# Queries in memory order of 1 KB pieces for batches 0 to 2, scores that read them with a step, and a new order of loads

## The chip, the core and the metric

One NeuronCore of a Trainium2 chip runs the whole program. The metric is the device time of one execution in microseconds (us), as the median of several runs. Engines: TensorE (matrix products, PE in the profile, its weight loads PEld), VectorE (DVE), ScalarE (ACT), GpSimd (POOL), and SP, which here only issues DMA transfers. The profile is one execution; its span is about 2 us below the time measured from outside.

## The reference, cut to what matters

Attention with a position bias over 8 batches of 8 heads, 576 tokens, 64 numbers a head, then layer norm and a two-layer MLP on each token:

```python
scores = scale * np.matmul(q, k.transpose(0, 1, 3, 2))
cum = np.cumsum(np.maximum(s, 0.0), axis=-1)
bias = -(cum[:, :, :, None] - cum[:, :, None, :])
scores = np.where(causal, -1e9, scores + np.minimum(bias, 0.0))
attn = softmax(scores);  x = attn @ v          # heads side by side: (8, 576, 512)
xn = (x - mu) / np.sqrt(var + 1e-06) * g_ln
out = x + np.maximum(xn @ w_ch1, 0.0) @ w_ch2  # 512 -> 2048 -> 512
```

## The kernel before

Heads are counted g = 0 to 63, eight a batch (b = g // 8). For a head, queries and keys are cast to bf16, turned by TensorE through an identity matrix into PSUM (the memory that matmuls write), and copied to `qkT`, with the bias as four extra rows (68 in all). The scores are computed with the keys as the stationary operand (the weight load, PEld in the profile) and the queries as the moving one, whose columns set the spacing of matmuls (in these traces 216 ns for 512 of them, some 30 for 64); ScalarE takes the exponential; TensorE multiplies with the values. The MLP of a finished batch is cut into units that fill TensorE between later heads.

Batches 1 and 2 (`QUADS`) load queries and keys in 1 KB pieces: partition p gets tokens 4p to 4p + 3. After the transposes column t * 128 + p holds token 4p + t, so the copy out of PSUM puts the columns in token order by reading with a step. Batch 0 is loaded in 256-byte pieces and needs no reordering.

```python
QUADS = (1, 2)
...
def t_quads(b, h, engs):                     # batches 1 and 2
    ...
        copy(
            engs[i],                         # queries (i = 0) and keys (i = 1)
            qkT[b][0:DK, i * H + h, 0 : NF * P].rearrange("r (p t) -> r p t", t=NF),
            pts[i][0:DK, 0 : NF * P].rearrange("r (t p) -> r p t", t=NF),
        )
    copy("dve", ..., tails[:, :, 0:TL])      # the last 64 tokens of both
...
def mm(o, kb, lo, hi):                       # scores of key block kb, queries lo to hi
    lhsT = qkT[b][0:DK, H + h, kb * P : (kb + 1) * P]
    ...
        nc.tensor.matmul(o[:, w:], lhsT=lhsT, rhs=qkT[b][0:DK, h, lo + w : hi], start=True, stop=True)

mm(s01[:, 0:512], 0, 0, 512)
mm(s01[:, 512:576], 0, 512, 576)
mm(s01[:, 576:1024], 1, 128, 576)
mm(s23[:, 0:320], 2, 256, 576)
mm(s23[:, 320:512], 3, 384, 576)
mm(pot[:, 448:512], 4, 512, 576)
...
for c, g in enumerate((6, 6, 7, 7)):                    # first weight
    at(g, "a", lambda c=c: load_w1(c))
for h, g in enumerate((0, 0, 1, 1, 7, 7, 8, 8)):        # heads of batch 1
    at(g, "e", lambda h=h: b1_in(h))
for i, g in enumerate((10, 10, 11, 11)):                # second weight
    at(g, "b", lambda i=i: load_w2(i))
```

The softmax here doesn't subtract the row's maximum and nothing guards it: scores larger than these inputs give would overflow.

## Time and profile before

| | before |
|---|---|
| median of 3 runs | 378.04 us (377.99 to 378.38) |
| TensorE busy | 94% of 378.5 us |
| VectorE, ScalarE, GpSimd busy | 53%, 43%, 44% |
| scores of g = 11 / g = 16 / g = 24 exponentiated from | 43.9 / 82.5 / 129.7 us |

TensorE's busy share is nearly all of the span, so what counts is where it is not full.

### The profile page before, as it was taken

What the parts mean: (1) busy time and instruction counts of PE and PEld (TensorE: products, weight loads), DVE (VectorE), ACT (ScalarE), POOL (GpSimd) and SP (SyncE); (2) the same over time, 40 slices, a digit from 0 to 9 for tenths busy, and PEclk for the clock granted to TensorE, in tenths of its full rate; (3) what the DMA queues carried; (4) which work ended last, traced back from release to release, by engine and by line L of the source; (5) the groups of instructions that cost most, each with busy time, mean ns of one, the idle gap of its engine ahead of it and who ended that gap; (6) DMA issues with size and microseconds to landing.
All of it is one profiled execution on the core that took longest, in us unless ns stands there. A gap on an engine that the chain in (4) does not pass through costs nothing.

```text
span 378.5 us, 7931 instructions
## 1 busy us (share of the span) xinstructions
PE 354.7 (94%) x3017; PEld 204.5 (54%) x3017; DVE 201.9 (53%) x466; ACT 163.9 (43%) x295; POOL 167.6 (44%) x328
## 2 busy tenths in 40 slices
PE   6987878888999999999999999999999999899994
PEld 5966645455555455545555755555555555344471
DVE  6788575765454544594447435733555353933131
ACT  3755755154563457335632546444623554031020
POOL 3537964493634545575455544463444111500000
PEclk9998999999999999999999999999999999999998
DMA  9958989997999789999999999599804001420202
GB/s 164 207 150 190 221 143 187 245 248 176 176 227 227 137 198 211 229 198 205 174 210 239 174 246 224 119 195 207 156 29 113 29 2 55 113 55 0 86 28 55
DMA packets 175253, 59.12 MB, mean 156 GB/s; under 512 B 162224, under 2 KB 170416, under 8 KB 175216
## 3 DMA queue, kind: packets, MB, share of 16 engines
q1 hardware_dynamic: 165200, 46.43, 63.5%
q0 software_dynamic: 4224, 4.19, 7.0%
q10 hardware_dynamic: 5792, 8.00, 6.3%
q8 instruction: 23, 0.38, 0.4%
q14 instruction: 14, 0.11, 0.1%
HBM read 37.11 MB, written 9.44 MB: 123 GB/s over the span
## 4 chain that ended last, share of the span: by engine, by line
PE 75%; DMA 11%; DVE 6%; SPq 4%; issue 2%; POOL 1%; ACT 0%; DVEq 0%; POOLq 0%; ACTq 0%
PE ph L373 29%; PE py L384 28%; PE s L217 9%; PE pot L264 6%; DMA ring<-in_q_dram 4%; DMA ring<-in_v_dram 4%; DVE xn L323 2%; SPq L430 2%; DMA ring<-in_k_dram 1%; DVE stats L308 1%; DMA xnT<-xn 1%; SPq L422 1%; SPq L434 1%; DVE x L273 1%; PE pt L186 1%
## 5 line engine op out<-in xcount | busy, mean ns | idle before, releaser
L233 ACT ACTIVATE e<-s 128x1024 bf16<-128x1024 f32 (+1 forms) x128 | 99.0, 808 | 88.0 <-PE s L217 86.2
L384 PE MATMUL py<-w_bf,hT 128*128 128x512 bf16 x576 | 133.4, 379 | 0.0
L373 PE MATMUL ph<-xnT,w_bf 128*128 128x512 bf16 x512 | 120.7, 379 | 1.7 <-DMA xnT<-xn 1.7
L236 POOL TENSOR_SCALAR_AFFINE_SELECT e<-e 128x384 bf16<-128x384 bf16 x104 | 45.7, 464 | 111.2 <-ACT e L233 102.6
L358 DVE TENSOR_SCALAR hT<-ph 128x512 bf16<-128x512 f32 x72 | 49.6, 690 | 77.0 <-PE ph L373 76.4
L373 PEld LDWEIGHTS <-w_bf 128*128 128x128 bf16 x640 | 58.2, 98 | 50.3 <-issue 2.2
L384 PEld LDWEIGHTS <-hT 128*128 128x128 bf16 x576 | 53.1, 98 | 56.1 <-DVE hT L358 0.2
L356 ACT ACTIVATE hT<-ph 128x512 bf16<-128x512 f32 x72 | 43.0, 597 | 79.6 <-PE ph L373 77.3
L217 PE MATMUL s<-qkT 68*128 68x64 bf16 (+5 forms) x320 | 54.5, 287 | 0.0
L127 POOL CAST aug<-ring 128x512 bf16<-128x512 f32 (+2 forms) x85 | 44.4, 547 | 15.0 <-DMA ring<-in_k_dram 7.3
L390 DVE SCALAR_TENSOR_TENSOR yo<-py,rstd,x 128x512 f32<-128x512 f32 x32 | 24.0, 749 | 47.7 <-PE py L384 45.5
L217 PEld LDWEIGHTS <-qkT 68*128 68x128 bf16 x372 | 32.5, 98 | 24.7
L264 PEld LDWEIGHTS <-e 128*128 128x128 bf16 x960 | 37.9, 98 | 13.6 <-POOL e L236 1.1
L264 PE MATMUL pot<-v_bf,e 128*128 128x65 bf16 x960 | 40.1, 194 | 1.4 <-POOL e L236 1.0
L273 DVE TENSOR_TENSOR x<-pot,rinv 128x320 f32<-128x320 f32 x64 | 31.5, 492 | 2.9 <-DMA out_dram<-yo 0.5
L125 DVE COPY qkT<-pt 68x512 bf16<-68x512 bf16 (+2 forms) x49 | 21.9, 468 | 12.5 <-PE pt L166 4.4
L308 DVE BATCH_NORM_STATS2 stats<-x 128x6 f32<-128x256 f32 (+2 forms) x68 | 23.4, 398 | 0.3
L323 DVE SCALAR_TENSOR_TENSOR xn<-x,mv,gln_b 128x512 bf16<-128x512 f32 x32 | 23.2, 766 | 0.0
L127 POOL CAST v_bf<-ring 128x512 bf16<-128x512 f32 (+2 forms) x33 | 19.5, 613 | 2.2 <-DMA ring<-in_v_dram 2.2
L272 DVE RECIPROCAL rinv<-pot 128x5 f32<-128x5 f32 x64 | 12.0, 187 | 15.0 <-PE pot L264 14.9
L329 POOL TENSOR_TENSOR rstd<-rstd,nhalf 128x2 f32<-128x2 f32 x18 | 18.6, 1031 | 1.5
L166 PE MATMUL pt<-ident,aug 128*68 128x128 bf16 x128 | 11.8, 226 | 6.8 <-POOL aug L127 3.1
(78 smaller groups left out, 217.8 us busy)
## 6 DMA issues: line engine op xcount, KB each, us to landing
out_dram<-yo ACTq DMA_DIRECT2D x27, 256.0 KB, 3.3
ring<-in_q_dram SPq DMA_DIRECT2D x20, 256.0 KB, 4.9
ring<-in_k_dram SPq DMA_DIRECT2D x20, 256.0 KB, 4.8
ring<-in_v_dram SPq DMA_DIRECT2D x20, 256.0 KB, 4.3
w_bf<-in_moe_w_ch_dram POOLq DMA_DIRECT2D x8, 512.0 KB, 9.7
ring<-in_k_dram SPq DMA_DIRECT2D x30, 128.0 KB, 4.2
ring<-in_q_dram SPq DMA_DIRECT2D x22, 128.0 KB, 4.7
x<-in_v_dram SPq DMA_DIRECT2D x17, 128.0 KB, 4.0
```

The costliest lines, as they stand in the source:

```text
L127: nc.gpsimd.tensor_copy(out=o, in_=i)
L217: nc.tensor.matmul(o[:, w:], lhsT=lhsT, rhs=qkT[b][0:DK, h, lo + w : hi], start=True, stop=True)
L233: nc.scalar.activation(out=o, in_=i, func=ACT.Exp, scale=scale)
L236: nc.gpsimd.affine_select(out=d, in_=d, compare_op=ALU.is_ge, fill=0.0, base=0, pattern=[[0, d.shape[1]], [1, P]], channel_multiplier=-1,)
L264: nc.tensor.matmul(pot[:, t * D1 : (t + 1) * D1], lhsT=e[:, c : c + P], rhs=v_bfs[b % 2][:, kb, h, :], start=(kb == 0), stop=(kb == t),)
L273: nc.vector.tensor_tensor(out=xs[b][:, :, h * D : (h + 1) * D], in0=pv[:, :, 0:D], in1=rv.to_broadcast([P, NT, D]), op=ALU.mult,)
L308: nc.vector.bn_stats(out=sts[c, a][:, part, :], in_=x_of(c, a)[:, lo:hi])
L323: eng.scalar_tensor_tensor(out=xn[:, j, :], in0=x_of(c, a), scalar=mv[:, j, 0:1], in1=gln_b, op0=ALU.subtract, op1=ALU.mult,)
L356: nc.scalar.activation(out=o, in_=i, func=ACT.Relu)
L358: nc.vector.tensor_scalar_max(out=o, in0=i, scalar1=0.0)
L373: nc.tensor.matmul(ph[:, j * tok : (j + 1) * tok], lhsT=w1_bf[:, kd, fb * P : (fb + 1) * P], rhs=xnT[c][:, :, kd, :], start=(kd == 0), sto ...
L384: nc.tensor.matmul(st["py"], lhsT=st["h"][:, fb, a * P : (a + 1) * P], rhs=w2_bf[:, fb, :], start=(fb == 0), stop=(fb == FB - 1),)
```

## The change

Its intent: batch 0 too in 1 KB pieces, which the DMA moves faster; spare VectorE the strided copy of the queries by letting TensorE read them in token order straight from the unordered columns; load batch 1 whole before the weights take the DMA; spread g over the partitions by a matmul rather than a broadcast load; issue the fifth score block after the next head's transposes. As the last 64 tokens stay in order, the score matmuls are also cut at token 512. The warm-up spin (matmuls on the identity matrix at the start that only keep TensorE busy) becomes fewer and wider matmuls, 11 of 512 columns for 44 of 128.

```diff
-    QUADS = (1, 2)
+    QUADS = (0, 1, 2)
...
+            if i == 0:
+                copy(engs[0], o[:, 0:S], pt[0:DK, 0:S])
+            else:
+                copy(engs[1], o[:, 0 : NF * P].rearrange("r (p t) -> r p t", t=NF), ...)
+                copy(engs[2], o[:, NF * P : S], pt[0:DK, NF * P : S])
...
+        def queries(lo, hi):
+            qT = qkT[b][0:DK, h, :]
+            if b in QUADS and hi <= NF * P:
+                qT = qT[:, 0 : NF * P].rearrange("r (t p) -> r p t", t=NF)
+                return qT[:, lo // NF : hi // NF]
+            return qT[:, lo:hi]
...
-        mm(pot[:, 448:512], 4, 512, 576)
+        return lambda: mm(pot[:, 448:512], 4, 512, 576)
...
-    spin(44)      # warm-up matmuls of 128 columns
+    spin(11)      # of 512 columns
...
+    def spread_g():
+        pg = ps_m.tile([P, 512], F32, name="pg", tag="pm")
+        nc.tensor.matmul(pg, lhsT=ones_r, rhs=gln_r, start=True, stop=True)
+        nc.vector.tensor_copy(out=gln_b, in_=pg)
...
-    for c, g in enumerate((6, 6, 7, 7)):
+    for c, g in enumerate((7, 7, 8, 8)):
         at(g, "a", lambda c=c: load_w1(c))
-    for h, g in enumerate((0, 0, 1, 1, 7, 7, 8, 8)):
+    for h, g in enumerate((1, 1, 1, 1, 3, 3, 3, 3)):
         at(g, "e", lambda h=h: b1_in(h))
-    for i, g in enumerate((10, 10, 11, 11)):
+    for i, g in enumerate((9, 9, 10, 10)):
         at(g, "b", lambda i=i: load_w2(i))
```

In `queries`, neighbours in the order of reading lie 128 elements, 256 bytes, apart.

More of the change, by code (lines that the diff above doesn't have):

```diff
@@ L97 @@
     xnT_tail = const.tile([P, 2, KD, P], BF16, name="xnT_tail")
+    gln_r, ones_r = xts[0][0:1, :], xts[2][0:1, Dm - P : Dm]
     scr = xbufs[0]
@@ L106 @@
     nc.sync.dma_start(out=s_sb, in_=s.rearrange("b h s -> (b h) s"))
+    nc.gpsimd.dma_start(out=gln_r, in_=moe_g_ln.rearrange("(o f) -> o f", o=1))
+    nc.gpsimd.memset(ones_r, 1.0)
     staged = {}
@@ L161, in t_quads @@
     def t_quads(b, h, engs):
-        pts = [ps_m.tile([P, 2 * 512], BF16, name="pt", tag="pm") for _ in range(2)]
-        tails = pts[1][0:DK, NF * P : NF * P + 2 * P].rearrange("r (j n) -> r j n", j=2)
         for i in range(2):
-            for p in range(NF):
+            pt = ps_m.tile([P, 2 * 512], BF16, name="pt", tag="pm")
+            o = qkT[b][0:DK, i * H + h, :]
+            for p in range(NT):
                 nc.tensor.transpose(
-                    pts[i][0:DK, p * P : (p + 1) * P], aug[:, p, i * H + h, 0:DK], ident
+                    pt[0:DK, p * P : (p + 1) * P], aug[:, p, i * H + h, 0:DK], ident
                 )
-            nc.tensor.transpose(tails[:, i, :], aug[:, NF, i * H + h, 0:DK], ident)
-            copy(
-                engs[i],
-                qkT[b][0:DK, i * H + h, 0 : NF * P].rearrange("r (p t) -> r p t", t=NF),
-                pts[i][0:DK, 0 : NF * P].rearrange("r (t p) -> r p t", t=NF),
-            )
-        copy(
-            "dve", qkT[b][0:DK, :, NF * P : S].rearrange("r (j h) n -> r j h n", j=2)[:, :, h, :],
-            tails[:, :, 0:TL],
-        )
-    def t_pe(b, h, engs=("dve", "dve")):
-        if b in QUADS:
-            return t_quads(b, h, engs)
-        for j, eng in ((h, engs[0]), (H + h, engs[1])):
-            pt = ps_m.tile([P, 2 * 512], BF16, name="pt", tag="pm")
-            for p in range(NT):
-                nc.tensor.transpose(pt[0:DK, p * P : (p + 1) * P], aug[:, p, j, 0:DK], ident)
-            copy(eng, qkT[b][0:DK, j, :], pt[0:DK, 0:SP_])
+            if i == 0:
+                copy(engs[0], o[:, 0:S], pt[0:DK, 0:S])
+            else:
+                copy(
+                    engs[1], o[:, 0 : NF * P].rearrange("r (p t) -> r p t", t=NF),
+                    pt[0:DK, 0 : NF * P].rearrange("r (t p) -> r p t", t=NF),
+                )
+                copy(engs[2], o[:, NF * P : S], pt[0:DK, NF * P : S])
     def t_dma(b, p):
@@ L203, in score_mms @@
         pots[g] = (pot, s01, s23)
+        def queries(lo, hi):
[4 more added lines that the diff above has]
+            return qT[:, lo:hi]
         def mm(o, kb, lo, hi):
             lhsT = qkT[b][0:DK, H + h, kb * P : (kb + 1) * P]
-            w = 0
+            cuts = {lo, hi}
+            if b in QUADS and lo < NF * P:
+                cuts.add(min(hi, NF * P))
             if g < NPM and lo == kb * P:
-                w = min(P, hi - lo)
-                nc.tensor.matmul(
-                    o[:, 0:w], lhsT=lhsT, rhs=qkT[b][0:DK, h, lo : lo + w], start=True, stop=False
-                )
-                nc.tensor.matmul(
-                    o[:, 0:w], lhsT=ident, rhs=negm[:, 0:w], start=False, stop=True
-                )
-            if lo + w < hi:
-                nc.tensor.matmul(
-                    o[:, w:], lhsT=lhsT, rhs=qkT[b][0:DK, h, lo + w : hi], start=True, stop=True
-                )
+                cuts.add(min(hi, lo + P))
+            cuts = sorted(cuts)
+            for c0, c1 in zip(cuts[:-1], cuts[1:]):
+                d = o[:, c0 - lo : c1 - lo]
+                m = g < NPM and c0 == kb * P
+                nc.tensor.matmul(d, lhsT=lhsT, rhs=queries(c0, c1), start=True, stop=not m)
+                if m:
+                    nc.tensor.matmul(
+                        d, lhsT=ident,
+                        rhs=negm[:, 0 : c1 - c0],
+                        start=False, stop=True,
+                    )
         mm(s01[:, 0:512], 0, 0, 512)
@@ L491, in spin @@
         for _ in range(n):
-            nc.tensor.matmul(idle[:, 0:P], lhsT=ident, rhs=ident, start=True, stop=True)
-    spin(44)
+            nc.tensor.matmul(
+                idle, lhsT=ident,
+                rhs=ident.rearrange("p (o n) -> p o n", o=1).to_broadcast([P, 4, P]),
+                start=True, stop=True,
+            )
+    spin(11)
     nc.vector.tensor_scalar(
@@ L501 @@
     )
-    pc = ps_m.tile([P, 512], F32, name="pc", tag="pm")
+    NQ = len(QUADS) * H
+    pq = ps_m.tile([P, 512], F32, name="pq", tag="pm")[:, 0 : NT * NQ]
+    pq = pq.rearrange("p (t c) -> p t c", t=NT)
+    cum_q = cum[0:NQ, 0 : NF * P].rearrange("c (p t) -> c t p", t=NF)
     for p in range(NT):
-        nc.tensor.transpose(pc[:, p * BH : (p + 1) * BH], cum[:, p * P : (p + 1) * P], ident_f)
+        nc.tensor.transpose(
+            pq[:, p, :], cum_q[:, p, :] if p < NF else cum[0:NQ, NF * P : SP_],
+            ident_f[0:NQ, 0:NQ],
+        )
     c8, r8 = (
@@ L507 @@
     )
-    pc_v = pc[:, 0 : NT * BH].rearrange("p (t c) -> p t c", c=BH)
     def split(lo, hi, eng, a=None, o=None):
@@ L521 @@
     cast_head("k", 0, 0, "pool")
-    split(0, H, nc.vector, pc_v[:, :, 0:H], aug[:, :, H:HD, D1:DK])
+    split(0, H, nc.vector, pq[:, :, 0:H], aug[:, :, H:HD, D1:DK])
     nc.scalar.activation(
@@ L527, with cum_all @@
     cast_head("k", 0, 1, "pool")
-    spin(8)
-    t_pe(0, 0, ("act", "dve"))
-    nc.scalar.copy(out=c8, in_=pc_v)
-    def cum_quads():
-        pq = ps_m.tile([P, 512], F32, name="pq", tag="pm")[:, 0 : NF * 3 * H]
-        pq = pq.rearrange("p (t c) -> p t c", t=NF)
-        cum_q = cum[0 : 3 * H, 0 : NF * P].rearrange("c (p t) -> c t p", t=NF)
-        for p in range(NF):
-            nc.tensor.transpose(pq[:, p, :], cum_q[:, p, :], ident_f[0 : 3 * H, 0 : 3 * H])
-        qs = slice(QUADS[0] * H, (QUADS[-1] + 1) * H)
-        nc.vector.tensor_copy(out=c8[:, 0:NF, qs], in_=pq[:, :, qs])
+    spin(2)
+    t_quads(0, 0, ("act", "dve", "act"))
+    nc.scalar.copy(out=c8[:, :, 0:NQ], in_=pq)
+    def cum_all():
+        pc = ps_m.tile([P, 512], F32, name="pc", tag="pm")
+        pc_v = pc[:, 0 : NT * BH].rearrange("p (t c) -> p t c", c=BH)
+        for p in range(NT):
+            nc.tensor.transpose(pc_v[:, p, :], cum[:, p * P : (p + 1) * P], ident_f)
+        nc.vector.tensor_copy(out=c8[:, :, NQ:BH], in_=pc_v[:, :, NQ:BH])
+    def spread_g():
+        pg = ps_m.tile([P, 512], F32, name="pg", tag="pm")
+        nc.tensor.matmul(pg, lhsT=ones_r, rhs=gln_r, start=True, stop=True)
+        nc.vector.tensor_copy(out=gln_b, in_=pg)
     cast_head("q", 0, 2, "dve")
@@ L567, in t_next @@
     def t_next(g):
-        t_pe((g + 2) // H, (g + 2) % H, ("dve", "act" if g >= H else "dve"))
-    at(0, "a2", lambda: t_pe(0, 1))
-    at(0, "a2", cum_quads)
+        t_quads((g + 2) // H, (g + 2) % H, ("dve", "act" if g >= H else "dve", "dve"))
+    at(0, "a2", lambda: t_quads(0, 1, ("dve", "dve", "dve")))
+    at(1, "c", cum_all)
+    at(3, "c", spread_g)
     at(2, "c", lambda: split(H, 2 * H, nc.vector))
@@ L589, in b1_in @@
     def b1_in(h):
-        if h == 2:
-            nc.sync.dma_start(out=gln_b, in_=moe_g_ln.partition_broadcast(P))
         heads_in(1, (h,))
@@ L605, in t_act @@
     def t_act(b, h):
-        t_pe(b, h, ("dve", "act"))
+        t_quads(b, h, ("dve", "act", "dve"))
     def c_head(b, h):
@@ L630 @@
         at(6 + p, "e", lambda p=p: nc.gpsimd.memset(aug[:, p, :, DK:P], 0.0))
+    B2 = 12
     def b2_in(g):
-        if g == 12:
+        if g == B2:
             for what in "qkv":
                 tails_in(what, 2, nc.sync)
-        heads_in(2, range(3 * (g - 12), min(H, 3 * (g - 12) + 3)))
-    for g in (12, 13, 14):
+        heads_in(2, range(3 * (g - B2), min(H, 3 * (g - B2) + 3)))
+    for g in (B2, B2 + 1, B2 + 2):
         at(g, "a", lambda g=g: b2_in(g))
@@ L711 @@
         if g < NG:
-            score_mms(g)
+            score_tail = score_mms(g)
             run(g, "a2")
+            score_tail()
             score_exp(g, 0)
```

## The prediction

> **What bounds the kernel now.** I read the page's slices first, then the matmuls in order of time, then the groups with shapes kept apart, then the DMA packets stretch by stretch.
>
> The slices (40 of 9.46 us each; a digit is the busy share in tenths):
> ```profile
> PE   6987878888999999999999999999999999899994
> DMA  9958989997999789999999999599804001420202
> ```
> From slice 11 (95 us) to slice 34 TensorE is full, and so is nearly all of the rest. Only the first ten slices have holes, and there DMA is full too, except in slices 3, 5 and 10. All the change's parts lie in batches 0 to 2 (heads g = 0 to 23), so the time can only be won or lost before some 95 us, and, where TensorE itself gets more work, up to g = 23.
>
> The holes, from the matmuls in order of time (start us, length us, then idle before and who ended it):
> ```profile
> 9.36 0.22 PE L210 MATMUL s<-qkT 68*128 68x128 bf16 x1 [1.13 <-ACT qkT L123]
> ...
> 32.69 0.41 PE L166 MATMUL pt<-ident,aug 128*68 128x128 bf16 x4 [1.30 <-POOL aug L127]
> ...
> 39.77 0.41 PE L166 MATMUL pt<-ident,aug 128*68 128x128 bf16 x4 [0.68 <-POOL aug L127]
> ...
> 44.09 1.89 PE L373 MATMUL ph<-xnT,w_bf 128*128 128x512 bf16 x8
> ...
> 56.50 0.38 PE L166 MATMUL pt<-ident,aug 128*68 128x128 bf16 x4 [1.95 <-DVE hT L358]
> ...
> 58.17 0.71 PE L264 MATMUL pot<-v_bf,e 128*128 128x65 bf16 x15 [0.96 <-POOL e L236]
> ...
> 73.83 0.40 PE L340 MATMUL ptx<-ident,xn 128*128 128x128 bf16 x4 [0.99 <-DVE xn L323]
> ...
> 91.92 0.38 PE L166 MATMUL pt<-ident,aug 128*68 128x128 bf16 x4 [1.34 <-DVE qkT L125]
> ```
> Scores of g = 0 start at 9.36, of g = 5 at 21.12, of g = 6 at 23.25: 2.13 to 2.3 us a head. Then g = 7 at 27.05, 8 at 29.29, 9 at 33.56, 10 at 37.37, 11 at 42.99. The extra 8 us there are waits for GpSimd's casts, which wait for batch 1's data. The MLP starts at 44.09. g = 16 starts at 80.43.
>
> A head of batch 0 costs TensorE 0.97 us of scores (9.36 to 10.33), 0.56 us of ten transposes and 0.46 us of values: 1.99 of its 2.13 us. So batch 0 already runs at TensorE's pace; DMA (24 loads of 128 KB, done by 20 us) is just behind.
>
> **What the skill says.** "DMA: Bandwidth & Descriptors", section "Why small descriptors are slow (HBM only)", gives a 256-byte descriptor 11 bus cycles for 8 of data, 27% overhead. The trace agrees in direction and shows more: in 10 to 20 us a 256-byte packet takes 20.8 ns (7777 packets) and a 1024-byte one 49.8 to 55 ns, so 1 KB costs 83 ns in small packets and some 52 in one.
> "TensorE: Matmul & The Clock Gate", section "Back-to-back issue gap", has N/2.4 + 2.5 ns warm. The trace agrees: eight 512-column matmuls take 1.73 us to the next one's start, 216 ns each.
> "SBUF — State Buffer", section "Specifications (TRN2)", says of the 16-byte lines "need ≥2 hits per line for full bandwidth; each cross to a new line pays a penalty". The new scores read one query, step 256 bytes, read the next: one hit per line. The kernel before has no strided moving operand, but it has a strided stationary one:
> ```profile
> 5.73 0.49 PE L504 MATMUL pc<-x 64*128 64x64 f32 x5 [0.18 <-DVE x L498]
> ...
> 10.98 0.65 PE L538 MATMUL pq<-x 24*128 24x24 f32 x4
> ```
> Taking off the last one's own length (223 and 272 ns), the contiguous loads follow each other every 0.066 us, and those with a step of 16 bytes every 0.12 us, though they have fewer rows and fewer columns to stream. That is twice as long and fits 128 reads at half of 2.4 GHz. No run yet shows it for a moving operand.
>
> **The change, part by part.**
>
> *Batch 0 in 1 KB pieces.* Its 16 q and k loads of 128 KB go from 512 packets x 20.8 ns / 16 = 0.67 us to 128 x 52 / 16 = 0.42 us: 4 us of DMA. Batch 0 is held by TensorE and the queue's issue (some 0.55 us a load), so its own pace gains nothing; batch 1 can start some 2 to 3 us sooner. The first scores wait on ScalarE's cast of head 1 and copy of head 0; the load lands some 0.6 us sooner, but the key's chain (a strided VectorE copy, then a tail copy) is 0.2 to 0.4 us longer. I take 9.3 us for the start, no gain.
>
> *The copies out of PSUM.* The groups (count | busy us, mean ns):
> ```profile
> L125 DVE COPY qkT<-pt 68x512 bf16<-68x512 bf16 x18 | 12.2, 681 | 4.6 <-PE pt L166 4.4
> L125 DVE COPY qkT<-pt 68x640 bf16<-68x640 bf16 x15 | 6.7, 481 | 3.8 <-PE pt L186 3.7
> L125 DVE COPY qkT<-pt 68x128 bf16<-68x128 bf16 x16 | 3.5, 217 | 4.1 <-ACT qkT L123 4.1
> ```
> A strided copy takes 681 ns, a plain one of 640 takes 481. Batch 0's heads go from two plain copies (0.96 us) to a plain one of 576 (0.44), a strided one and a tail (0.2): 1.32 us. With reciprocal and multiply (0.68) VectorE has 2.0 us a head by summed means, some 1.8 when the overlap of neighbours is taken off. It comes close to being the bound in g = 0 to 10 but does not pass 2.5 us. From g = 8 on a head saves VectorE 0.24 us.
>
> *Scores by strides.* Of a head's 1600 columns 1280 lie below token 512 (512 + 384 + 256 + 128) and are read with the step. At full speed they are 1280 / 2.4 = 0.53 us; at half speed 1.07. So +0.53 us a head if the rule seen on the stationary side holds here, 12.8 us of TensorE for 24 heads, and nothing if it doesn't. The cuts at token 512 add two 64-column matmuls a head in batch 0 (three from g = 12), some 5 ns each, as a 65-column one takes 0.46 / 15 = 31 ns against 27 of columns: 0.3 us in all.
>
> *Batch 1 ahead of the weights.* Before, heads 4 to 7 are issued from 32.05 to 43 us, beside the first weight (issued at 33.0), and the last value tile is waited for until 51.6. After, 30 loads at 0.53 us follow batch 0's directly: issued some 16 to 33 us, head 0 landed near 21, head 4 near 31, head 7 near 36. TensorE wants head 0 at g = 6 (23 to 26 us) and head 4 at g = 10 (36). So these waits go. The first weight is then issued at about 28, the second at about 36; 13.4 us of DMA each (2048 packets x 105 ns / 16), done near 44 and 58. Batch 2, whose tails wait for the last cast of batch 1 (at 55.46 before), starts near 42 and has all landed by about 71 instead of 80.
>
> *The fifth score block after the transposes*, and g by a matmul: the first takes away waits of 0.1 to 0.4 us on VectorE's multiply; the second costs one fp32 matmul (0.9 us estimated as four passes of 512 columns) and one 0.69 us PSUM copy, and removes a 256 KB load.
>
> **The sum.** With the penalty, TensorE's work for g = 0 to 10: 2.6 + 2.8 (the 40-column cumulative sums) + 2.5 + 3.35 (g) + 5 x 2.5 + 2.5 + 3.4 (x transposes) = 29.7 us, so g = 11 at 39.0, and 40.5 with VectorE's stalls: 2.5 us gained. From g = 11 to 18 the waits of 0.96 (GpSimd behind a late value tile), 0.99 (VectorE behind a late query of batch 2) and part of 1.34 and 0.67 go: 3.5 gained. The 1.95 stays: it is VectorE's split of batches 2 to 7. Lost: 5 x 0.53 = 2.65 in g = 11 to 15, and 3.5 to 4.2 in g = 16 to 23, where TensorE is the bound. Total about 0: 378 us.
> Without the penalty, g = 11 comes at about 38 (VectorE and TensorE nearly equal), 5 us gained, plus the same 3.5: 369.5 us.
>
> **The rivals.** (1) *The step is free for moving operands.* For it: separate read paths for moving and stationary data, and nothing in the trace of a strided moving read. Against: the doubled stationary loads, and the skill's line on cache lines. It gives 367 to 372. (2) *The step costs double and TensorE's gain is eaten*: 375 to 381, the likelier one, about 0.7. (3) *VectorE becomes the bound of batch 0* through the three copies: g = 5 at 23 or later and 2 to 3 us of the gain lost even without a penalty, 371 to 374. Against it: 0.6 us of VectorE idle per head before. (4) *The transfers are late anyway*: the early second weight shares DMA with batch 2, so q and k of batch 2 are not sooner than TensorE gets there; then the 3.5 us shrink to 1 to 2. For it: DMA is at 9 in most of slices 4 to 12.
>
> **Range and chances.** Weighing 378 at 0.7 and 369.5 to 372 at 0.3 gives 376. The range 369.5 to 380.5 spans both cases with 2.5 us outside either middle where I think it likely. 2% is 7.6 us, that is below 370.5: only rival 1 in its better half, with nothing lost to VectorE: 0.24. Slower by over 2% needs a step worse than double: 0.04.
>
> **What would show it.** Right: the 68x384 and 68x512 score matmuls last 0.16 to 0.21 us longer, and a head's scores 1.47 us instead of 0.97 (g below 12), 1.22 instead of 0.68 (from 12); no waits over 0.3 us on GpSimd's casts between g = 6 and 11; g = 11 between 38 and 41; the last batch 1 value cast by 40, not 52; strided PSUM copies of queries gone. Wrong: if score matmuls keep their lengths, the result is below 372; if g = 5 starts after 24 with TensorE idle behind VectorE, rival 3; if GpSimd or VectorE still wait for batch 2's loads at g = 15, rival 4.

## The result, and the profile after

The changed kernel takes 412.56 us (median of 4 runs, 411.94 to 413.48) against 378.21 us beside it: the ratio is 1.0907, with a 95% interval of 1.0878 to 1.0935. It is slower by 9%. Here and below a ratio is the mean time of one kernel's runs over that of the other's from the same rounds, so it is not quite the ratio of the medians. Executions over 1.5% slower than the fastest of the same kernel are left out of the means.

The slices of the changed kernel's page (40 of 10.28 us; PEclk is the clock granted to TensorE, in tenths of full speed):

```profile
PE   7999999998999999999999999999999999989995
PEclk9557999999999999999999999999999999999998
```

The holes in TensorE's first ten slices are nearly gone, as intended, and yet all is later. TensorE is not waiting: it is busy for 397 us instead of 355. The second row shows a thing that I had not foreseen: the clock is at half from slice 2 to some way into slice 4 (9.2 to 36.5 us), while TensorE is full.

The groups of score matmuls with their shapes kept apart, before and after (count | busy us, mean ns | idle before):

```profile
L217 PE MATMUL s<-qkT 68*128 68x512 bf16 x52 | 19.8, 381 | 0.0
L217 PE MATMUL s<-qkT 68*128 68x384 bf16 x12 | 4.1, 343 | 0.0
```

```profile
L216 PE MATMUL s<-qkT 68*128 68x512 bf16 x52 | 27.6, 531 | 0.0
L216 PE MATMUL s<-qkT 68*128 68x384 bf16 x24 | 19.6, 816 | 0.0
L216 PE MATMUL s<-qkT 68*128 68x256 bf16 x24 | 14.4, 599 | 0.0
L216 PE MATMUL s<-qkT 68*128 68x448 bf16 x40 | 14.1, 351 | 0.0
```

The 384-column matmuls went from 343 to 816 ns. The 512-column group mixes 12 stepped ones with the 40 of batches 3 to 7: if those 40 stayed at 381, the 12 took (52 x 531 - 40 x 381) / 12 = 1031 ns. The 448-column ones, now only of batches 3 to 7 and without a step, kept their 351.

One head of batch 1 in TensorE's order of time, after and before (start us, length us):

```profile
71.26 2.45 PE L216 MATMUL s<-qkT 68*128 68x512 bf16 x8
73.55 0.19 PE L216 MATMUL pot<-qkT 68*128 68x64 bf16 x1
73.58 1.89 PE L376 MATMUL ph<-xnT,w_bf 128*128 128x512 bf16 x8
```

```profile
47.69 0.82 PE L217 MATMUL s<-qkT 68*128 68x512 bf16 x5
48.34 0.19 PE L217 MATMUL pot<-qkT 68*128 68x64 bf16 x1
```

From the first score matmul to the fifth block the head takes 2.29 us, and took 0.65: 1.64 us more, at full clock, beside the same MLP units (eight of 512 columns in 1.73 us to the next start, as before). 24 heads make 39 us of added TensorE work (an estimate from this head; heads below g = 12 are cut differently, and one at full clock, g = 7, takes 2.5 us from its first score matmul to the transposes, where such a head of e2 below takes 0.9).

The progress of four kernels, as the start of ScalarE's first exponential of a head in their profiles (us). The last two columns are of experiments told below:

| head | before | after | same reads without the step (e2) | queries by copies (e8) |
|---|---|---|---|---|
| g = 0 | 10.1 | 11.5 | 10.7 | 10.2 |
| g = 8 | 30.1 | 49.0 | 31.0 | 30.7 |
| g = 11 | 43.9 | 61.1 | 41.2 | 41.7 |
| g = 16 | 82.5 | 103.4 | 75.5 | 75.5 |
| g = 24 | 129.7 | 162.2 | 121.8 | 122.1 |
| span | 378.5 | 411.3 | 371.2 | 373.2 |

The loss of 32.5 us is complete at g = 24, and from there to the end the kernel before and the changed one both need 249 us.

### The profile page after: what moved, and what is told of

It reads as the page before. It is cut to its first block, busy times and chain, and to the rows that moved or that the text cites. A ratio compares the mean times of both kernels' runs of the same rounds, so it can differ in the third digit from the quotient of the medians.

```text
span 411.3 us, 7966 instructions
## 1 busy us (share of the span) xinstructions
PE 397.2 (97%) x3014; PEld 214.4 (52%) x3041; DVE 199.2 (48%) x474; ACT 164.9 (40%) x296; POOL 168.4 (41%) x331
## 4 chain that ended last, share of the span: by engine, by line
PE 89%; DVE 5%; POOL 1%; issue 1%; DMA 1%; ACT 1%; ACTq 0%; DVEq 0%; POOLq 0%
PE ph L376 30%; PE py L387 25%; PE s L216 20%; PE pot L267 7%; PE pt L170 4%; DVE xn L326 1%; PE idle L495 1%; DVE stats L311 1%; DMA xnT<-xn 1%; PE s L218 1%; DVE yo L393 1%; POOL aug L131 1%; ACT e L236 1%; DVE x L276 1%; PE pg L554 0%
## 5 line engine op out<-in xcount | busy, mean ns | idle before, releaser
L387 PE MATMUL py<-w_bf,hT 128*128 128x512 bf16 x549 | 130.8, 381 | 1.4
L216 PE MATMUL s<-qkT 68*128 68x64 bf16 (+7 forms) x428 | 95.4, 358 | 0.8 <-DVE qkT L129 0.8
L216 PEld LDWEIGHTS <-qkT 68*128 68x128 bf16 x492 | 45.1, 105 | 59.9 <-issue 30.7
L267 PE MATMUL pot<-v_bf,e 128*128 128x65 bf16 x960 | 41.2, 197 | 0.0
L129 DVE COPY qkT<-pt 68x576 bf16<-68x576 bf16 (+2 forms) x56 | 20.2, 383 | 31.2 <-PE pt L170 25.2
L170 PE MATMUL pt<-ident,aug 128*68 128x128 bf16 x240 | 21.2, 246 | 1.7 <-DVE qkT L129 1.0
L170 PEld LDWEIGHTS <-aug 128*68 128x68 bf16 x240 | 18.3, 132 | 4.2 <-issue 1.8
L275 DVE RECIPROCAL rinv<-pot 128x5 f32<-128x5 f32 x64 | 12.0, 187 | 14.5 <-PE pot L267 14.4
```

What stands on the lines that cost most here:

```text
L170: nc.tensor.transpose(pt[0:DK, p * P : (p + 1) * P], aug[:, p, i * H + h, 0:DK], ident)
L216: nc.tensor.matmul(d, lhsT=lhsT, rhs=queries(c0, c1), start=True, stop=not m)
L267: nc.tensor.matmul(pot[:, t * D1 : (t + 1) * D1], lhsT=e[:, c : c + P], rhs=v_bfs[b % 2][:, kb, h, :], start=(kb == 0), stop=(kb == t),)
L387: nc.tensor.matmul(st["py"], lhsT=st["h"][:, fb, a * P : (a + 1) * P], rhs=w2_bf[:, fb, :], start=(fb == 0), stop=(fb == FB - 1),)
```

## The experiments

Theory A: the step in the moving operand costs TensorE about four times the time per column, and the half clock is a consequence. Theory B: the new warm-up spin leaves the clock at half, and the step carries only part of the loss. (That spin has as many columns, and its first part runs for 4.6 us where the old one ran for 4.0.) A third possibility was that VectorE's three copies a head hold up batch 0; the changed kernel's own list of waits speaks against it, with 1.8 us of TensorE's waits for these copies up to g = 24.

**The same matmuls without the step (e2).** Instruction for instruction the changed kernel; only the addresses of the moving reads differ. Its results are wrong; the bias is set to zero so that the exponentials stay finite.

```diff
-                return qT[:, lo // NF : hi // NF]
+                return qkT[b][0:DK, h, lo:hi]
```

> The changed kernel, instruction for instruction, but the scores read the same number of queries without the step (and the bias terms are set to 0 so that nothing overflows): wrong on purpose. Theory A (the step costs about four times the time per column, and TensorE's half clock from 9 to 36 us is only its consequence): 366 to 374 us, score matmuls of 512 columns back to 381 ns from 531, the clock full from some 6 us on. Theory B (the new, shorter warm-up spin leaves the clock at half, and the step itself costs only part of the loss): the clock still at half from 9 to about 36 us and 376 to 390 us.

Measured: 374.51 us (372.94 to 375.92; ratio to before 0.9906, interval 0.9868 to 0.9944). The step is worth the whole loss: the medians differ by 38.1 us and the profiles' spans by 411.3 - 371.2 = 40.1 (e2's profile is of its fastest run), against 39 us from 24 heads at 1.64. The lengths are back:

```profile
L216 PE MATMUL s<-qkT 68*128 68x512 bf16 x52 | 19.8, 381 | 0.0
L216 PE MATMUL s<-qkT 68*128 68x384 bf16 x24 | 7.9, 329 | 0.0
```

The time is just above the range that theory A gave; for the step the mechanism was A's. Of the clock A had said "full from some 6 us on"; it was at half for 3.4 us (10.3 to 13.8), not 27. The table also shows how the lost time adds up. At g = 8 the changed kernel is 18.0 us behind this one: 8 heads x 1.64 = 13 us, and 5 us more, while its clock is at half. At g = 24 it is 40.4 us behind, 39 of which are the step. So the half clock cost some 5 us in batch 0 by this estimate. That so little of it shows at g = 24 fits with TensorE's waits: from 9 us to g = 24 they sum to 7.6 us in e2 and to 3.8 in the changed kernel.

**The old spin in the changed kernel (e3).**

```diff
-    spin(11)     # and spin(2), of 512 columns
+    spin(44)     # and spin(8), of 128 columns
```

> The changed kernel with the warm-up spin of before (44 and 8 matmuls of 128 columns). Theory A: the clock is still at half from about 9 to 36 us, 409 to 413 us. Theory B: the clock stays full and the time falls by 6 us or more, to 400 to 406 us.

Measured: 412.25 us (two runs), no change. Windows of 10 us of the changed kernel, then of this one (busy us of each engine, then the granted clock, the DMA share and GB/s):

```profile
10.00:20.00 10.00, 10.00 (x84) 7.55 (x82) 4.10 (x11) 3.48 (x6) 6.17 (x15) 0.50 0.86 216
20.00:30.00 10.00, 10.00 (x86) 7.47 (x86) 5.64 (x16) 3.47 (x6) 5.62 (x14) 0.50 0.69 179
```

```profile
10.00:20.00 10.00, 10.00 (x89) 6.61 (x88) 4.32 (x12) 3.42 (x6) 6.54 (x16) 0.83 0.85 216
20.00:30.00 10.00, 10.00 (x83) 6.37 (x82) 5.47 (x15) 3.42 (x6) 6.08 (x14) 0.58 0.75 193
```

The old spin moves the half-clock stretches about (this profile has another from 59.2 to 62.6) but doesn't end them; TensorE counts as busy for the full 10 us in all four. With e2, which has the new spin and only 3.4 us of half clock, theory B falls. This profile also prices the half clock: 10.2 us less of it before g = 8 puts that head 2.2 us ahead of the changed kernel, and g = 24 still 2.1.

What lets the clock fall is not shown, and so A's second half is not shown either. The longest stretches at half lie in stepped matmuls of batch 0 (27 us in the changed kernel, 17 here and in e7 below). But the changed kernel is back at full clock from 36.5 us, while its stepped matmuls go on to g = 23, with only 3.4 us more at half; and shorter stretches come without any step, such as 6.8 us in e10 and 10.2 us in e4's copy of the kernel before, ahead of its probes.

**The price of a step by itself (e4).** The kernel before, with matmuls of 512 columns behind its end that read the first weight in several ways.

```diff
+    quad = flat[:, 0:512].rearrange("p (t n) -> p n t", t=4)
+    pair = flat[:, 0:512].rearrange("p (t n j) -> p n t j", t=4, j=2)
+    # 12 x flat[:, 0:512]; then 6 each of steps 2, 4, 8, 16, of quad, of pair, and step 1 again:
+    nc.tensor.matmul(probe, lhsT=ident, rhs=..., start=True, stop=True)
```

> The kernel before with matmuls of 512 columns put behind its end, which read a bf16 operand with a step of 1, 2, 4, 8, 16 elements, in fours 256 bytes apart as the changed scores do, and in pairs of neighbours 256 bytes apart. Only the spacing of these matmuls counts, not the time of the kernel. If what counts is one hit per 16-byte line: 216 ns for steps 1, 2 and 4, some 850 ns (four times) for 8, 16 and the fours, about half of that for the pairs. If any step costs: 850 ns for step 2 and 4 too. If the cost comes from hopping among four places: the fours alone are slow.

The order of time, one line for each kind (start us, length us; L735 is step 1, L737 step 2, L739 step 4, L741 step 8, L743 step 16, L745 the fours of the change, L747 pairs, L749 step 1 again):

```profile
371.82 2.75 PE L735 MATMUL probe<-w_bf,ident 128*128 128x512 bf16 x12
374.41 1.52 PE L737 MATMUL probe<-w_bf,ident 128*128 128x512 bf16 x6
375.77 2.87 PE L739 MATMUL probe<-w_bf,ident 128*128 128x512 bf16 x6
378.46 5.58 PE L741 MATMUL probe<-w_bf,ident 128*128 128x512 bf16 x6
383.86 5.69 PE L743 MATMUL probe<-w_bf,ident 128*128 128x512 bf16 x6
389.36 5.36 PE L745 MATMUL probe<-w_bf,ident 128*128 128x512 bf16 x6
394.55 2.80 PE L747 MATMUL probe<-w_bf,ident 128*128 128x512 bf16 x6
397.17 2.67 PE L749 MATMUL probe<-w_bf,ident 128*128 128x512 bf16 x6
```

From the start of one matmul to the next, in the middle of each group (single records of the trace, which the lines merge): 216 ns for step 1, 227 for step 2, 452 for step 4, 900 for step 8, 918 for step 16, 864 for the fours, 437 for the pairs. So neither "any step costs" (step 2 is nearly free) nor "one hit per line" (step 4 has two elements in 16 bytes and costs double) as I had written it. What fits is a price for each 16-byte line that the read turns to: step 8 turns to 512 lines in 900 ns, 1.76 ns a line; step 4 to 256, which gives 450; step 2 to 128, 225; step 1 to 64, 113, which hides behind the 216 that 512 columns take anyway. The clock was at half from 382.6 us on, and step 8 took 900 ns on either side of that; the fours took 864 here, at half, and 864 again in the next experiment at full clock: the price does not depend on TensorE's clock. It also explains the changed kernel: (2.29 - 4 x 0.03 for the unstepped blocks in that time) / 1280 columns = 1.70 ns a column, close to the fours' 864 / 512 = 1.69.

**The rule put to the test (e9).** Another set behind the same kernel: pairs, runs of four neighbours, a step of 3; then stationary operands, contiguous and with a step of 8.

```diff
+    runs4 = flat[:, 0:512].rearrange("p (t n j) -> p n t j", t=4, j=4)
+    # ... 6 x pairs, runs4, flat[:, 0:1536:3]; then, with 64 moving columns:
+    nc.tensor.matmul(probe[:, 0:64], lhsT=flat[:, 0:128], rhs=ident[:, 0:64], start=True, stop=True)
+    nc.tensor.matmul(probe[:, 0:64], lhsT=flat[:, 0:1024:8], rhs=ident[:, 0:64], start=True, stop=True)
```

> The kernel before with another set of matmuls behind its end: 512 columns read in pairs of neighbours 256 bytes apart, in runs of four neighbours 256 bytes apart, with a step of 3 elements; then 64-column matmuls whose stationary operand of 128 bf16 columns is contiguous, and with a step of 8 elements; then plain ones and the fours again. If a moving read costs some 1.75 ns for each 16-byte line it turns to (900 ns / 512): pairs 448 ns at full clock, runs of four 224 or the plain 216, step 3 (192 lines) some 336. If any break in the run costs, runs of four are well above 216. The stationary operand: 31 ns contiguous; 120 ns with the step if it goes at the rate of the fp32 loads of the kernel before (128 reads), 224 if at the moving operand's.

In order of time (L736 pairs, L738 runs of four, L740 step 3, L742 and L744 the stationary operands, L746 step 1, of which the trace lacks the first record, L748 the fours):

```profile
371.57 2.78 PE L736 MATMUL probe<-w_bf,ident 128*128 128x512 bf16 x6
374.18 1.51 PE L738 MATMUL probe<-w_bf,ident 128*128 128x512 bf16 x6
375.53 2.20 PE L740 MATMUL probe<-w_bf,ident 128*128 128x512 bf16 x6
377.56 0.52 PE L742 MATMUL probe<-ident,w_bf 128*128 128x64 bf16 x12
377.91 0.91 PE L744 MATMUL probe<-ident,w_bf 128*128 128x64 bf16 x12
378.88 1.24 PE L746 MATMUL probe<-w_bf,ident 128*128 128x512 bf16 x5
379.96 3.61 PE L748 MATMUL probe<-w_bf,ident 128*128 128x512 bf16 x4
```

Start to start, at full clock: pairs 437 ns (448 expected), runs of four 222 (224), step 3 340 (336). The rule holds in all three. With the stationary operand the matmuls follow each other after 29 ns, and after 62 with a step of 8: twice as long, and only 0.5 ns for each of the 128 columns loaded. (The 64 moving columns alone take 27 ns at 216 for 512, so the 29 may be theirs and not the load's.) Neither of the two values that I had expected came, but it shows why my prediction could not carry the price over: the same step that makes this spacing 2.1 times as long makes that of a moving read 4.2 times as long.

**The change without the step: queries by strided copies (e1, e8).** All of the change stays except that VectorE orders the queries again, as it did in batches 1 and 2.

```diff
-                copy(engs[0], o[:, 0:S], pt[0:DK, 0:S])
+            copy(engs[i], qkT[b][0:DK, i * H + h, 0 : NF * P].rearrange("r (p t) -> r p t", t=NF), ...)
+        copy(engs[2], ..., tails[:, :, 0:TL])
...
-            if b in QUADS and hi <= NF * P:
+            if False:
```

> The changed kernel, but the queries are put in order by the strided copy out of PSUM, as batches 1 and 2 had it before, and the scores read them without a step; all else of the change stays (right results). Theory A: the loss goes and the rest of the change shows its worth: 368 to 376 us, the clock full from 6 us. Rival (VectorE becomes the bound of batch 0 with two strided copies a head): 376 to 382 us, with TensorE waiting on VectorE's copies in g = 1 to 6. Theory B: half clock until some 36 us and 380 to 390 us.

Measured: correct, median of the five fast runs 375.68 us (375.71 with the slow one), ratio of the fast runs 0.9906 (0.9874 to 0.9937). The profiled run took 952 us: in it a head with four MLP units took 12.5 us instead of 4.6, with TensorE busy throughout and no clock change on record. It was run again:

> The kernel of e1_query_copies once more, because its profile fell in a run of 952 us. Expected: 373 to 376 us as its five other runs, TensorE's work for a head of batch 1 or 2 as in the kernel before (0.68 us of scores), and VectorE nearly full in g = 0 to 10 if it is what now bounds that stretch. If the 952 us come again, they belong to the kernel and not to the chip's state.

Measured: 374.27 us (373.68 to 376.68), ratio 0.9894 (0.9863 to 0.9925), and no run like the odd one in six. So this version beats both kernels, the kernel before by 1% (clear of noise, but under the 2% that counts as faster here). What may keep it from gaining more is in the windows (columns as above, VectorE the third):

```profile
20.00:30.00 10.00, 8.68 (x162) 7.59 (x160) 9.84 (x28) 6.73 (x12) 7.65 (x16) 1.00 0.81 189
30.00:40.00 10.00, 6.86 (x128) 6.00 (x126) 9.77 (x31) 7.08 (x13) 9.10 (x16) 1.00 1.18 205
```

VectorE is busy for 9.8 of 10 us from 20 to 40 us. TensorE's waits between 9 and 122 us are now mostly for VectorE (the longest in total of this kernel, then of the kernel before to 130 us; us, times, longest):

```profile
PE pot L218 <- DVE x L278: 3.4, 5, 1.5
PE pt L170 <- DVE qkT L129: 1.4, 2, 1.0
```

```profile
PE pt L166 <- POOL aug L127: 3.1, 5, 1.3
PE pt L166 <- DVE hT L358: 1.9, 1, 1.9
```

GpSimd's casts, which waited for data, are gone from TensorE's list. VectorE took their place. The waits of the two full lists together fall from 14.4 to 8.9 us, 5.5 less, and the spans differ by 5.3.

**The order of loads alone (e5)**, in the kernel before:

```diff
-    for c, g in enumerate((6, 6, 7, 7)):
+    for c, g in enumerate((7, 7, 8, 8)):
-    for h, g in enumerate((0, 0, 1, 1, 7, 7, 8, 8)):
+    for h, g in enumerate((1, 1, 1, 1, 3, 3, 3, 3)):
-    for i, g in enumerate((10, 10, 11, 11)):
+    for i, g in enumerate((9, 9, 10, 10)):
```

> The kernel before with nothing but the new order of loads (batch 1 whole from g = 1 and 3, the weights at g = 7 and 8, and 9 and 10). If the order is what the change gains: 374 to 376 us, with the waits on GpSimd's casts in g = 7 to 11 mostly gone. If the gain needs batch 0's 1 KB pieces first (batch 1 cannot start sooner than 18 us): 376.5 to 378.5 us, the waits at g = 6 and 7 still there.

Measured: 376.21 us, ratio 0.9939 (0.9912 to 0.9967). In its profile g = 11 comes at 41.3 and g = 16 at 77.3, against 41.7 and 75.5 with all the rest. More than half of the gain seems to be the order; the rest of the change together (1 KB pieces of batch 0, fifth block, spin, g) adds what remains, by times whose intervals overlap.

**g by a DMA again (e6)**, in the version with copies (the load of the kernel before is put back, the matmul and its copy taken out):

```diff
-    at(3, "c", spread_g)
+        if h == 2:
+            nc.sync.dma_start(out=gln_b, in_=moe_g_ln.partition_broadcast(P))
```

> The kernel of e1_query_copies, but g is spread by a DMA again as before. If spreading g by TensorE costs its two fp32 matmuls (some 1 us at full clock) and its 0.68 us copy on the path of batch 0: 0.8 to 1.5 us faster than e8, 372.5 to 375 us. If those lie beside waits, or the 256 KB load delays batch 1 by as much: within 0.4 us of e8.

Measured: 375.58 us, ratio 0.9918 (0.9895 to 0.9940), against 0.9894 for e8. The expected gain of a microsecond did not come. The two intervals overlap, so I can only say that spreading g by TensorE costs nothing that shows.

**The step in batch 0 alone (e7)**, batches 1 and 2 by copies:

```diff
+    STEP = (0,)
-            if b in QUADS and hi <= NF * P:
+            if b in STEP and hi <= NF * P:
```

> The step only in the scores of batch 0, batches 1 and 2 by strided copies as in e1. If every head pays the same 1.6 us: 8 x 1.6 = 13 us over e8, 387 to 390 us. If batch 0 has slack for it (VectorE's copies, waits for data): 380 to 385 us. The clock at half for much of 10 to 35 us if the stepped matmuls cause it.

Measured: three runs of 388.07, 391.51 and 393.89 us (a fourth, of 394.04, slow), ratio 1.0333 (1.0277 to 1.0389). The profiled run is the fastest, with a span of 386.3 us, 13.1 over e8's 373.2. That this is just 8 heads x 1.64 is partly luck: at g = 24 it is 15.1 us behind e8, with 17 us of half clock where e8 had none, and the rest of e8's profile has 3.4 us of half clock that this one has not. The other runs lie above the 390 that I had allowed. They have no profile, but their granted clock falls as the time grows: 0.974 in the profiled run, 0.959 at 391.51, 0.956 at 393.89. So batch 0 did not hide the step, as my second guess had it: TensorE's listed waits up to g = 24 only fall from 8.9 us in e8 to 7.5.

**Taking load off VectorE (e10, e11, e12).** In the version with copies, the key copy goes to ScalarE from g = 4, or from g = 1, instead of g = 8:

```diff
-        t_quads((g + 2) // H, (g + 2) % H, ("dve", "act" if g >= H else "dve", "dve"))
+        t_quads((g + 2) // H, (g + 2) % H, ("dve", "act" if g >= 4 else "dve", "dve"))
```

> The kernel of e1/e8 with the strided key copy on ScalarE from g = 4 instead of g = 8. In e8 VectorE is busy for 9.8 of 10 us from 20 to 40 us and TensorE waits on its multiply. If VectorE bounds that stretch: four copies of 0.6 us less, g = 11 some 2 us sooner, 372 to 373.5 us against e8's 374.3. If ScalarE (6.7 of 10) then makes the scores wait for its exponentials: no change or slower.

> The same with the key copy on ScalarE from g = 1. ScalarE then has 1.7 us of exponentials and 0.6 us of copy a head, more than TensorE's 2.0 us: it becomes the bound, 373 to 376 us, not better than e10.

Measured: 378.18 us (ratio 0.9991) and 377.81 us (1.0009; five runs; a sixth, of 383.34, slow): the gain over the kernel before is lost. In e10's profile heads 4 to 7 start 3.2 us apart, and TensorE waits for ScalarE each time:

```profile
28.83 0.22 PE L218 MATMUL s<-qkT 68*128 68x128 bf16 x1 [1.08 <-ACT e L238]
```

In ScalarE's part of the program the key copy stood before the exponentials of the head, so those waited for transposes that TensorE does after the scores. Not all of e10's loss is the edit's, though: its profile has 6.8 us of half clock from 9.2 us on, and at g = 3, before anything edited runs, it is already 2.7 us behind e8; from there to g = 11 it loses 2.7 more. The last run puts the transposes behind the exponentials from g = 4:

```diff
-            at(g, "a2" if g < H else "b", lambda g=g: t_next(g))
+            at(g, "a2" if g < 4 else "b", lambda g=g: t_next(g))
```

> As e10, but from g = 4 the transposes of the next head come after the head's exponentials, as they do from g = 8, so that ScalarE's key copy no longer stands between a head's scores and its exponentials. In e10 TensorE waited 1.07 us a head for the exponentials of g = 4 to 7. If that order was e10's fault: those waits go and VectorE's relief shows, 372 to 374 us, at or below e8. If ScalarE is simply full: 375 to 378 us.

Measured: 376.49 us, ratio 0.9926, and a wrong result (relative error 0.064). By the program's order the cause is my edit: at g = 5 the bias of batch 1 is written into the buffer that all batches share, at the same place in the order and before the transposes of batch 0's last head. This was read from the code and not tested. The 1.07 us waits are gone, so they came of the order; yet the time is no better than e8's. So that VectorE's load is what holds e8 back is read from its trace, and no run confirms it: none that took work off VectorE came under e8. Differences of 1 us between these versions also lie within what the clock does: e8's own runs go from 373.7 us at a granted clock of 0.997 to 376.7 at 0.986.

## Why the prediction was wrong

I said 376.0 us, within 369.5 to 380.5, and the kernel takes 412.56.

*The step that failed* is the term "+0.53 us a head" under "Scores by strides". It measured 1.64 us a head. I had seen that a step matters, and found the right place, but I took the factor of two from strided weight loads of the kernel before, and e4 and e9 show that a moving read pays another price: 4.2 times for a step of 8, where the spacing with a strided weight load grows 2.1 times. Even the reading was loose: (0.65 - 0.272) / 3 is 0.126 us, not 0.12, and 128 reads at half of 2.4 GHz make 0.107. The rule that I drew from the skill, one hit per line or two, was too kind as well: it takes four bf16 neighbours of a 16-byte line to be at full speed. The sum was then 12.8 us where it is 39. The sentence "Slower by over 2% needs a step worse than double: 0.04" names what happened and gives it far too little, for a factor that I had from another operand.

*The half clock* appears nowhere in the prediction. By the comparison with e2 it cost some 5 us by g = 8; at g = 24 the difference to e2 is 1 us more than the step. Its cause stays open.

*The rest without the step* I put at 369.5 to 372 us; e2 measured 374.5. The term that was too large is "g = 11 comes at about 38 ... 5 us gained": by the same measure, the head's first score matmul, it came at 40.0, 3.0 us before the kernel before. That looks like rival 3, which gave 371 to 374 us: VectorE, which I had at 1.8 to 2.0 us a head, is busy for 9.4 of 10 us from 20 to 40 in e2. The second term, 3.5 us from g = 11 to 18, was too small, if anything: that takes 46.0 us in e2 and 51.0 before. The term for the 1 KB pieces was too large: such a packet took 72 ns in the mean from 0 to 10 us of the changed kernel and 58 from 10 to 20, not 52.

*Right:* the holes on GpSimd's casts between g = 6 and 11 went, also with the order of loads alone (e5); the heads' scores were the thing to look at; no gain at the start; the cuts at token 512 cost nothing that shows. *Wrong in detail:* I had the last value cast of batch 1 by 40 us; in e8 it still waits for its load and starts at 51.99. That load, issued at 36.6, shares the DMA with the two weights, issued from 27.8 on. So "these waits go" holds for TensorE and not for GpSimd.

## What to carry to other kernels

The order in which a moving operand is read has a price on TensorE: count the 16-byte lines that the read turns to, and compare that with its columns. A permutation that costs VectorE 0.2 us in a copy can cost TensorE 1.6 us when it is folded into the matmuls, and it is paid again in each matmul that reads the data. The order of reads may be free again where runs of neighbours are long enough (four bf16 numbers here). A ratio seen on one operand or engine should not be moved to another: put ten matmuls behind the end of the kernel and measure it.

## What the Trainium skill lacked or had wrong

- "SBUF — State Buffer", section "Specifications (TRN2)": "need ≥2 hits per line for full bandwidth". For TensorE's moving operand in bf16 two hits are not enough: step 4 and pairs take 452 and 437 ns for 512 columns against 216. Four are (step 2: 227, runs of four: 222). The page gives no price; here it is 1.7 to 1.8 ns a line, the same at half clock.
- "TensorE: Matmul & The Clock Gate", section "Weight-path perf modes — Fast Weight Load (FWL) and DoubleRow", lists weights "packed or strided" without a price for the step. With 64 moving columns a matmul whose stationary operand has a step of 8 elements follows after 62 ns instead of 29 (e9).
- The same page, section "Part 1: The HAM clock gate", lets activity release the throttle and idle time bring it back. Here the clock stood at half for 27 us (9.2 to 36.5) while TensorE counted as busy, from 9.5 us without a gap, in stepped matmuls; e2, the same instructions without the step, had 3.4 us of it. Why is not shown: stepped matmuls ran at full clock later in the same run.
- "DMA: Bandwidth & Descriptors", section "Why small descriptors are slow (HBM only)", gives 27% overhead for 256 bytes. Here the gap depends on what one takes: in the kernel before, from 10 to 20 us, 1 KB took 83 ns in four packets and 50 in one (of which there were only 52); in the changed kernel, in the same stretch, 72 and 58 (3262 packets of 256 bytes and 1280 of 1 KB), 23% more.
